# Retention and a two-layer MLP in one kernel: q and k loaded by GpSimd ahead of the weights, v from SyncE, k cast by VectorE, token groups of 512 and 256, first group alone

## Chip, cores, metric

One core of a Trainium2 chip. The metric is the device time of one execution in microseconds (us); medians of several runs are quoted. Names in profile lines: PE is TensorE, DVE VectorE, ACT ScalarE, POOL GpSimd, SP SyncE; L178 is line 178 of that run's kernel, so one statement has different line numbers in different kernels.

## The reference

```python
# q, k, v: (8 batches, 8 heads, 576 tokens, 64)
scores = (1/8) * q @ k^T                       # per batch and head
ret    = scores * gamma[h] ** (i - j)  for i >= j, else 0
x      = (ret @ v) as (4608 tokens, 512)
h      = x @ w_in                              # 512 x 2048
out    = max(0.01 * h, h) @ w_out              # 2048 x 512
```

Inputs and output are f32; the kernel computes in f16 with f32 sums.

## The kernel before

The attention part works on 40 *units*: 128 tokens of one batch (64 for the last of each batch), all 8 heads. Its steps are short, and they are dealt out between the long blocks of the two MLP layers. VectorE lays v and k out block-diagonally (`vdiag`, `kstk`), PE transposes q and k (`tr`; VectorE and ScalarE copy k from there into `kdiag`), and states (`ups`, `sinit`, `sdiag`), scores (`sc`, `s`) and outputs (`ot`) follow. ScalarE copies each output into `xT`, the input of the first MLP layer, whose matmuls write `hps`; those of the second write `yps`.

```python
def load(u):                       # q and k, f32, from SyncE
    for x, t_ap in enumerate((q, k)):
        t = ld_pool.tile([P, H, D], FP, name=f"qk32_{x}")    # 4 buffers
        nc.sync.dma_start(out=t[0:n], in_=...)

def load_v(b):                     # v of a whole batch, cast to f16 by the DMA, 8 DMAs
    nc.gpsimd.dma_start(out=t[...], in_=v[b, ...])

def cast(u):                       # q and k to f16, times decay table
    for x in range(2):
        eng = nc.vector if (u < 5 and x == 1) else nc.gpsimd
        eng.tensor_tensor(out=t[0:n], in0=qk32[u, x][0:n], in1=<table>, op=MUL)

def st_transpose(u):
    <2 vdiag copies, 4 kstk copies, on VectorE, f16 SBUF to SBUF>
    <8 transposes on PE; qT and half of kdiag on ScalarE; half of kdiag on VectorE>

def s0():                          # first step of unit u
    load(u + 4)
    if w == 1: load_v(b + 1)
    cast(u + 2)
    st_transpose(u)
# further steps: st_state(u, 0), st_scores(u), st_state(u, 1), st_out(u)
...
# start: load(0), load_v(0), load(1..3), cast(0), cast(1), then 4 w_in and 4 w_out
# loads on GpSimd (f32 to f16). Nine groups of 512 tokens: group g's first layer runs
# beside group g-1's second layer and the units of group g+1.
```

Of the kernel before, what the change touches and what calls it, by code (L numbers as in the profile page):

```python
# [10 lines left out]
FP = mybir.dt.float32  # L11
F16 = mybir.dt.float16
# [6 lines left out]
def kernel(  # L19
# [16 lines left out]
    nc = tc.nc  # L36
    B, H, S, D = q.shape
    NT, DM = out.shape
    DFF = moe_w_in.shape[1]
    P = 128  # L40
    CH = 64
    BLK = 3 * CH
    NP = H // 2
    NI = S // CH
    NF = DFF // P
    TOK = 512
    NG = NT // TOK
# [18 lines left out]

    const_pool = ctx.enter_context(tc.tile_pool(name="const", bufs=1))
    ld_pool = ctx.enter_context(tc.tile_pool(name="ld", bufs=4))
    v_pool = ctx.enter_context(tc.tile_pool(name="vp", bufs=2))
    a_pool = ctx.enter_context(tc.tile_pool(name="ap", bufs=3))  # L70
    g_pool = ctx.enter_context(tc.tile_pool(name="gp", bufs=2))
    o_pool = ctx.enter_context(tc.tile_pool(name="op", bufs=4))
    tr_pool = ctx.enter_context(tc.tile_pool(name="trp", bufs=1, space=PSUM))
# [3 lines left out]
    h_pool = ctx.enter_context(tc.tile_pool(name="hpp", bufs=2, space=PSUM))  # L77
    y_pool = ctx.enter_context(tc.tile_pool(name="yp", bufs=2, space=PSUM))
# [12 lines left out]
    xT = const_pool.tile([P, NP, NT], F16, name="xT")  # L91
    w_in16 = const_pool.tile([P, NP, DFF], F16, name="w_in16")
    w_out16 = const_pool.tile([P, NF, DM], F16, name="w_out16")

    NZ = 2
# [4 lines left out]
    sdiags = [const_pool.tile([P, NP, P], F16, name=f"sdiag{z}") for z in range(NS)]  # L100
    halves = [const_pool.tile([P, H, D], F16, name=f"half{x}") for x in range(2)]

    vst = {}

    def load_v(b):
        t = v_pool.tile([P, NP, NI, D], F16, name="vst")
        vst[b] = t
        for p in range(NP):
            for hh in range(2):
                nc.gpsimd.dma_start(  # L110
                    out=t[CH * hh : CH * hh + CH, p, :, :],
                    in_=v[b, 2 * p + hh].rearrange("(i s) d -> s i d", s=CH),
                )

    units = [(b, w) for b in range(B) for w in range((S + P - 1) // P)]
    NU = len(units)
    nrows = [min(P, S - P * w) for b, w in units]
    qk32 = {}
    qk16 = {}

    def load(u):
        b, w = units[u]
        n = nrows[u]
        for x, t_ap in enumerate((q, k)):
            t = ld_pool.tile([P, H, D], FP, name=f"qk32_{x}")
            qk32[u, x] = t
            nc.sync.dma_start(
                out=t[0:n],
                in_=t_ap[b, :, P * w : P * w + n, :].rearrange("h t d -> t h d"),
            )  # L130

    def cast(u):
        b, w = units[u]
        n = nrows[u]
        for x in range(2):
            if n == P:
                t = a_pool.tile([P, H, D], F16, name=f"qk16_{x}")
            else:
                t = halves[x]
            qk16[u, x] = t  # L140
            eng = nc.vector if (u < 5 and x == 1) else nc.gpsimd
            eng.tensor_tensor(  # L142
                out=t[0:n],
                in0=qk32[u, x][0:n],
                in1=tab_sb[0:n, w % 3, x, :].unsqueeze(2).to_broadcast([n, H, D]),
                op=MUL,
            )

    qTs = {}
    s16s = {}  # L150
# [5 lines left out]
    def st_transpose(u):  # L156
        b, w = units[u]
        n = nrows[u]
        nb = n // CH
        z = u % NZ  # L160
        for hh in range(2):
            nc.vector.tensor_copy(  # L162
                out=vdiags[z][CH * hh : CH * hh + CH, :, 0:nb, CH * hh : CH * hh + CH],
                in_=vst[b][CH * hh : CH * hh + CH, :, 2 * w : 2 * w + nb, :],
            )
        k16 = qk16[u, 1].rearrange("s (p h) d -> s p h d", h=2)
        if not (w == 4):
            for j in range(nb):
                for hh in range(2):
                    nc.vector.tensor_copy(  # L170
                        out=kstks[z][CH * hh : CH * hh + CH, :, j, CH * hh : CH * hh + CH],
                        in_=k16[CH * j : CH * j + CH, :, hh, :],
                    )
        tr = tr_pool.tile([P, 2, NP, P], F16, name="tr")
        for x in range(2):
            for p in range(NP):
                nc.tensor.transpose(  # L177
                    tr[:, x, p, :],  # L178
                    qk16[u, x][:, 2 * p : 2 * p + 2, :].rearrange("t h d -> t (h d)"),
                    ident,  # L180
                )
        qT = a_pool.tile([P, NP, P], F16, name="qT")
        qTs[u] = qT
        nc.scalar.copy(out=qT[:, :, 0:n], in_=tr[:, 0, :, 0:n])  # L184
        for hh, eng in ((0, nc.scalar.copy), (1, nc.vector.tensor_copy)):
            eng(  # L186
                out=kdiags[z][CH * hh : CH * hh + CH, :, 0:nb, CH * hh : CH * hh + CH],
                in_=tr[CH * hh : CH * hh + CH, 1, :, 0:n].rearrange(
                    "e p (j c) -> e p j c", c=CH
                ),  # L190
            )

    def st_state(u, j):
        b, w = units[u]
        z = u % NZ
# [6 lines left out]
        for p in range(NP):  # L202
            nc.tensor.matmul(  # L203
                out=ut[:, p, :],
                lhsT=kstks[z][:, p, j, :],
                rhs=vst[b][:, p, i, :],
                start=(i % 3 == 0 and p == 0),
                stop=(i % 3 == 2),
                skip_group_check=True,
            )  # L210
# [54 lines left out]
    def st_out(u):  # L265
# [19 lines left out]
        t0 = b * S + P * w  # L285
        nc.scalar.copy(out=xT[:, :, t0 : t0 + n], in_=ot[:, :, 0:n])  # L286

    def slots(u):

        b, w = units[u]  # L290

        def s0():
            if u + 4 < NU:
                load(u + 4)
            if w == 1 and b + 1 < B:
                load_v(b + 1)
            if u + 2 < NU:
                cast(u + 2)
            st_transpose(u)

        yield s0
        yield lambda: st_state(u, 0)
        yield lambda: st_scores(u)
        if nrows[u] == P:
            yield lambda: st_state(u, 1)
        yield lambda: st_out(u)
# [7 lines left out]
        nc.vector.memset(sdiags[z], 0.0)  # L314
    for x in range(2):
        nc.vector.memset(halves[x], 0.0)
    load(0)
    load_v(0)
    for u in range(1, 4):
        load(u)  # L320
    cast(0)
    cast(1)
    FQ = DFF // 4
# [8 lines left out]
            in_=moe_w_out[c * FQ : (c + 1) * FQ, :].rearrange("(c k) f -> k c f", k=P),  # L332
        )

    first_slot = []
    need = []
    for u in range(NU):
        b, w = units[u]
        lo = b * NI + 2 * w
        for s in slots(u):  # L340
            first_slot.append(s)
            need.append(lo // 8)
    done = 0

    g_tiles = {}

    def g1(g, fc):
        if fc == 0:
            g_tiles[g] = g_pool.tile([P, NF, TOK], F16, name="gt")
        hps = h_pool.tile([P, TOK], FP, name="hps")  # L350
        for c in range(NP):
            nc.tensor.matmul(  # L352
                out=hps,
                lhsT=w_in16[:, c, fc * P : (fc + 1) * P],
                rhs=xT[:, c, g * TOK : (g + 1) * TOK],
                start=(c == 0),
                stop=(c == NP - 1),
            )
        nc.scalar.activation(  # L359
            out=g_tiles[g][:, fc, :], in_=hps,  # L360
            func=mybir.ActivationFunctionType.Lrelu,
        )

    y_cur = {}

    def g2(g, n):
        tb, part = n // 4, n % 4
        if part == 0:
            y_cur[g] = y_pool.tile([P, DM], FP, name="yps")
        for f in range(4 * part, 4 * part + 4):  # L370
            nc.tensor.matmul(  # L371
                out=y_cur[g],
                lhsT=g_tiles[g][:, f, tb * P : (tb + 1) * P],
                rhs=w_out16[:, f, :],
                start=(f == 0),
                stop=(f == NF - 1),
            )
        if part == 3:
            osb = o_pool.tile([P, DM], FP, name="osb")
            nc.vector.tensor_copy(out=osb, in_=y_cur[g])  # L380
            r0 = g * TOK + tb * P
            nc.sync.dma_start(out=out[r0 : r0 + P, :], in_=osb)

    def run_slots(upto):
        nonlocal done
        while done < upto:
            first_slot[done]()
            done += 1

    total = len(first_slot)  # L390
    ends = [sum(1 for x in need if x <= g) for g in range(NG)] + [total]
    run_slots(ends[0])
    for g in range(NG + 1):
        a = done
        e = ends[min(g + 1, NG)] if g < NG else total
        nblk = (16 if g < NG else 0) + (16 if g > 0 else 0)
        m = 0
        for n in range(NF):
            if g < NG:
                g1(g, n)  # L400
                m += 1
                run_slots(a + (e - a) * m // nblk)
            if g > 0:
                g2(g - 1, n)
                m += 1
                run_slots(a + (e - a) * m // nblk)


# [28 lines left out]
```

## Time and profile before

| | before |
|---|---|
| median of 3 runs | 366.6 us |
| span of the profiled run | 364.9 us |
| first matmul of the first MLP layer (hps) | 50.5 us |
| PE packed from | 81.4 us |
| VectorE busy | 198.1 us |

"Packed" means that PE waits for almost nothing: from 82 us to the end it waited 5.3 us. The prediction below shows the lines for this and how they are read. A line for a group of instructions has busy time in us and mean duration in ns behind the first bar, and the idle time before them behind the second.

### The profile page before, as it was taken

The page shows a single profiled execution, that of the slowest core. Times are in us where ns is not written, and L with a number is a line of the kernel's source. Part 1 is how long each engine was busy: PE and PEld are TensorE (multiplying, and loading weights), DVE is VectorE, ACT ScalarE, POOL GpSimd, SP SyncE. Part 2 cuts the span into 40 slices and gives each one's busy share as a digit, 9 for nine tenths or more (in the row PEclk, how much of TensorE's full clock was granted, in tenths as well). Part 3 has the DMA queues.
Part 4 walks back from the last instruction along what each step waited for, and adds up shares of the span by engine and source line. Part 5 has one row for each costly group of instructions (what it writes and reads, how often), then busy time and mean ns, then how long its engine had stood idle before and what let it go on. Part 6 is the DMA issues. An engine that isn't in the chain of part 4 may idle for free.

```text
span 364.9 us, 6523 instructions
## 1 busy us (share of the span) xinstructions
PE 311.6 (85%) x2560; PEld 168.9 (46%) x2560; DVE 198.1 (54%) x492; ACT 144.2 (40%) x266; POOL 131.4 (36%) x153
## 2 busy tenths in 40 slices
PE   0024278779999999999999999999999999999995
PEld 0023144445554555555555555555555455544442
DVE  5448248782656577636756775445884556300021
ACT  1111046354444455434444444444445444433300
POOL 9822379426322573166225822373132100000000
PEclk9999999899999999999999999999999999999999
DMA  9999999709335393387338943593452000011012
GB/s 158 189 196 196 176 192 182 126 3 78 91 78 128 90 189 89 88 118 93 86 88 156 125 103 77 129 152 88 105 113 73 31 29 32 29 44 44 29 62 84
DMA packets 122479, 37.71 MB, mean 103 GB/s; under 512 B 113744, under 2 KB 117840, under 8 KB 122448
## 3 DMA queue, kind: packets, MB, share of 16 engines
q1 hardware_dynamic: 80192, 28.32, 35.2%
q0 software_dynamic: 42112, 8.92, 27.3%
q8 instruction: 20, 0.33, 0.4%
q10 hardware_dynamic: 144, 0.06, 0.1%
q14 instruction: 11, 0.09, 0.1%
HBM read 36.76 MB, written 9.44 MB: 127 GB/s over the span
## 4 chain that ended last, share of the span: by engine, by line
PE 78%; DMA 7%; DVE 6%; POOL 4%; ACT 2%; issue 2%; POOLq 0%; DVEq 0%
PE yps L371 34%; PE hps L352 32%; DMA w_out<-in_moe_w_out_dram 7%; PE tr L177 4%; PE ot L275 2%; PE sc L242 2%; PE ot L280 2%; POOL vst L110 2%; PE ups L203 2%; ACT xT L286 1%; DVE kstk L170 1%; POOL qk L142 1%; POOL w_in L325 1%; DVE s L253 1%; DVE sdiag L233 1%
## 5 line engine op out<-in xcount | busy, mean ns | idle before, releaser
L352 PE MATMUL hps<-xT,w_in 128*128 128x512 f16 x576 | 149.9, 383 | 5.9 <-ACT xT L286 5.9
L371 PE MATMUL yps<-w_out,gt 128*128 128x512 f16 x576 | 145.2, 379 | 0.0
L359 ACT ACTIVATE gt<-hps 128x512 f16<-128x512 f32 x144 | 86.0, 597 | 133.0 <-PE hps L352 131.8
L142 POOL TENSOR_TENSOR qk<-qk,cs 128x512 f16<-128x512 f32 x60 | 62.5, 1059 | 117.0 <-DMA qk<-in_q_dram 39.5
L371 PEld LDWEIGHTS <-gt 128*128 128x128 f16 x576 | 52.8, 98 | 54.6
L352 PEld LDWEIGHTS <-w_in 128*128 128x128 f16 x576 | 51.0, 99 | 51.7 <-issue 8.1
L110 POOL DMA_DIRECT2D vst<-in_v_dram x64 | 47.5, 775 | 32.8 <-DMA w_out<-in_moe_w_out_dram 11.4
L380 DVE COPY osb<-yps 128x512 f32<-128x512 f32 x36 | 24.9, 691 | 51.3 <-PE yps L371 51.0
L186 DVE COPY kdiag<-tr 64x512 f16<-64x512 f16 (+1 forms) x40 | 16.0, 401 | 59.5 <-ACT kdiag L186 59.2
L286 ACT CAST xT<-ot 128x512 f16<-128x512 f32 (+1 forms) x40 | 21.6, 541 | 40.9 <-PE ot L280 40.9
L203 PE MATMUL ups<-vst,kstk 128*128 128x64 f16 x256 | 18.9, 199 | 21.1 <-DVE kstk L170 11.7
L170 DVE COPY kstk<-qk 64x256 f16<-64x256 f16 x128 | 34.2, 267 | 3.0
L177 PE MATMUL tr<-ident,qk 128*128 128x128 f16 x256 | 21.5, 232 | 15.8 <-POOL qk L142 15.8
L203 PEld LDWEIGHTS <-kstk 128*128 128x128 f16 x256 | 16.4, 102 | 35.6 <-DVE kstk L170 22.2
L184 ACT COPY qT<-tr 128x512 f16<-128x512 f16 (+1 forms) x40 | 21.6, 540 | 27.6 <-PE tr L177 27.6
L233 DVE TENSOR_TENSOR sdiag<-ups,sinit 64x256 f16<-64x256 f32 x64 | 26.9, 421 | 4.2 <-PE ups L203 3.3
L177 PEld LDWEIGHTS <-qk 128*128 128x128 f16 x256 | 18.2, 104 | 22.3 <-POOL qk L142 15.9
L162 DVE COPY vdiag<-vst 64x512 f16<-64x512 f16 (+1 forms) x80 | 27.0, 337 | 1.5
L253 DVE TENSOR_TENSOR s<-sc,cs 128x512 f16<-128x512 f32 x32 | 22.1, 691 | 9.0 <-PE sc L242 8.4
L275 PE MATMUL ot<-s,vdiag 128*128 128x64 f16 x288 | 23.0, 199 | 2.6 <-DVE s L253 2.6
L275 PEld LDWEIGHTS <-vdiag 128*128 128x128 f16 x288 | 20.9, 102 | 5.6 <-issue 1.0
L280 PE MATMUL ot<-qT,sdiag 128*128 128x64 f16 x256 | 22.0, 200 | 0.0
(30 smaller groups left out, 154.0 us busy)
## 6 DMA issues: line engine op xcount, KB each, us to landing
out_dram<-osb SPq DMA_DIRECT2D x36, 256.0 KB, 2.2
qk<-in_q_dram SPq DMA_DIRECT2D x32, 256.0 KB, 4.3
qk<-in_k_dram SPq DMA_DIRECT2D x32, 256.0 KB, 4.4
vst<-in_v_dram POOLq DMA_DIRECT2D x64, 72.0 KB, 5.0
w_in<-in_moe_w_in_dram POOLq DMA_DIRECT2D x4, 512.0 KB, 12.5
w_out<-in_moe_w_out_dram POOLq DMA_DIRECT2D x4, 512.0 KB, 23.3
qk<-in_q_dram SPq DMA_DIRECT2D x8, 128.0 KB, 4.7
qk<-in_k_dram SPq DMA_DIRECT2D x8, 128.0 KB, 4.4
```

Of the source, the lines that this page charges most:

```text
L110: nc.gpsimd.dma_start(out=t[CH * hh : CH * hh + CH, p, :, :], in_=v[b, 2 * p + hh].rearrange("(i s) d -> s i d", s=CH),)
L142: eng.tensor_tensor(out=t[0:n], in0=qk32[u, x][0:n], in1=tab_sb[0:n, w % 3, x, :].unsqueeze(2).to_broadcast([n, H, D]), op=MUL,)
L162: nc.vector.tensor_copy(out=vdiags[z][CH * hh : CH * hh + CH, :, 0:nb, CH * hh : CH * hh + CH], in_=vst[b][CH * hh : CH * hh + CH, :, 2 * ...
L170: nc.vector.tensor_copy(out=kstks[z][CH * hh : CH * hh + CH, :, j, CH * hh : CH * hh + CH], in_=k16[CH * j : CH * j + CH, :, hh, :],)
L177: nc.tensor.transpose(tr[:, x, p, :], qk16[u, x][:, 2 * p : 2 * p + 2, :].rearrange("t h d -> t (h d)"), ident,)
L203: nc.tensor.matmul(out=ut[:, p, :], lhsT=kstks[z][:, p, j, :], rhs=vst[b][:, p, i, :], start=(i % 3 == 0 and p == 0), stop=(i % 3 == 2), s ...
L233: nc.vector.tensor_tensor(out=dst, in0=ut[lo:hi], in1=sins[b][lo:hi], op=ADD)
L275: nc.tensor.matmul(out=o, lhsT=vdiags[z][:, p, j, :], rhs=s16s[u][:, p, j, :], start=True, stop=(i == 0),)
L280: nc.tensor.matmul(out=o, lhsT=sdiag_at[b, i][:, p, :], rhs=qTs[u][:, p, CH * j : CH * j + CH], start=False, stop=True,)
L352: nc.tensor.matmul(out=hps, lhsT=w_in16[:, c, fc * P : (fc + 1) * P], rhs=xT[:, c, g * TOK : (g + 1) * TOK], start=(c == 0), stop=(c == NP ...
L359: nc.scalar.activation(out=g_tiles[g][:, fc, :], in_=hps, func=mybir.ActivationFunctionType.Lrelu,)
L371: nc.tensor.matmul(out=y_cur[g], lhsT=g_tiles[g][:, f, tb * P : (tb + 1) * P], rhs=w_out16[:, f, :], start=(f == 0), stop=(f == NF - 1),)
```

## The change

The intent: let the first units' data come ahead of the 4.2 MB of weights, no longer block GpSimd behind the weight loads, and let the first 512 tokens go through both layers alone while the other loads arrive.

```diff
+    def load_qk(u):
...
-            nc.sync.dma_start(
+            nc.gpsimd.dma_start(
...
+    def load_v(u):                              # per unit, f32, four (or two) DMAs
+                nc.sync.dma_start(out=t[...], in_=v[b, ...])
...
     def cast(u):
-            eng = nc.vector if (u < 5 and x == 1) else nc.gpsimd
+            eng = nc.gpsimd if (u >= 4 and x == 0) else nc.vector
...
+        nc.scalar.copy(out=t[:, :, 0:nb, :], in_=v32[u][:, :, 0:nb, :])    # v to f16
...
+    def prepare(u):
+        if u + 2 < NU:
+            cast(u + 2)
+        if u + 4 < NU:
+            load_qk(u + 4)
+        if 4 <= u + 3 < NU:
+            load_v(u + 3)
+        st_transpose(u)

     def slots(u):
+        if u == 0:
+            yield lambda: prepare(0)
         yield lambda: st_state(u, 0)
         yield lambda: st_scores(u)
+        if u + 1 < NU:
+            yield lambda: prepare(u + 1)
         if nrows[u] == P:
             yield lambda: st_state(u, 1)
         yield lambda: st_out(u)
...
+    sizes = [512, 256, 256] + [512] * 6 + [256, 256]
...
+    run_steps(ends[0])
+    run(ends[0], g1_blocks(0))                  # first layer of the first group, alone
+    run(ends[1], g2_blocks(0, 2))               # its second layer, with units 4 to 6
+    run(ends[2], g1_blocks(1))
+    for g in range(2, NG):
+        run(ends[g + 1], g1_blocks(g), g2_blocks(g - 1))
+    run(ends[NG], g2_blocks(NG - 1))
```

The pool of f16 tiles also goes from 3 to 4 buffers.

More of the change, by code (lines that the diff above doesn't have):

```diff
@@ L68 @@
     ld_pool = ctx.enter_context(tc.tile_pool(name="ld", bufs=4))
-    v_pool = ctx.enter_context(tc.tile_pool(name="vp", bufs=2))
-    a_pool = ctx.enter_context(tc.tile_pool(name="ap", bufs=3))
+    a_pool = ctx.enter_context(tc.tile_pool(name="ap", bufs=4))
     g_pool = ctx.enter_context(tc.tile_pool(name="gp", bufs=2))
@@ L101 @@
     halves = [const_pool.tile([P, H, D], F16, name=f"half{x}") for x in range(2)]
-    vst = {}
-    def load_v(b):
-        t = v_pool.tile([P, NP, NI, D], F16, name="vst")
-        vst[b] = t
-        for p in range(NP):
-            for hh in range(2):
-                nc.gpsimd.dma_start(
-                    out=t[CH * hh : CH * hh + CH, p, :, :],
-                    in_=v[b, 2 * p + hh].rearrange("(i s) d -> s i d", s=CH),
-                )
     units = [(b, w) for b in range(B) for w in range((S + P - 1) // P)]
@@ L119 @@
     qk16 = {}
-    def load(u):
+    v32 = {}
+    vst = {}
+    def load_qk(u):
         b, w = units[u]
@@ L130, in load @@
             )
+    def load_v(u):
+        b, w = units[u]
+        t = ld_pool.tile([P, NP, 2, D], FP, name="v32")
+        v32[u] = t
+        for j in range(nrows[u] // CH):
+            t0 = P * w + CH * j
+            for hh in range(2):
+                nc.sync.dma_start(
+                    out=t[CH * hh : CH * hh + CH, :, j, :],
+                    in_=v[b, :, t0 : t0 + CH, :].rearrange(
+                        "(p h) s d -> h s p d", h=2
+                    )[hh],
+                )
     def cast(u):
@@ L134, in cast @@
         n = nrows[u]
+        nb = n // CH
+        z = u % NZ
         for x in range(2):
@@ L147, in cast @@
             )
+        t = a_pool.tile([P, NP, 2, D], F16, name="vst")
+        vst[u] = t
+        nc.scalar.copy(out=t[:, :, 0:nb, :], in_=v32[u][:, :, 0:nb, :])
     qTs = {}
@@ L163, in st_transpose @@
                 out=vdiags[z][CH * hh : CH * hh + CH, :, 0:nb, CH * hh : CH * hh + CH],
-                in_=vst[b][CH * hh : CH * hh + CH, :, 2 * w : 2 * w + nb, :],
+                in_=vst[u][CH * hh : CH * hh + CH, :, 0:nb, :],
             )
@@ L205, in st_state @@
                 lhsT=kstks[z][:, p, j, :],
-                rhs=vst[b][:, p, i, :],
+                rhs=vst[u][:, p, j, :],
                 start=(i % 3 == 0 and p == 0),
@@ L286, in st_out @@
         nc.scalar.copy(out=xT[:, :, t0 : t0 + n], in_=ot[:, :, 0:n])
-    def slots(u):
-        b, w = units[u]
-        def s0():
-            if u + 4 < NU:
-                load(u + 4)
-            if w == 1 and b + 1 < B:
-                load_v(b + 1)
-            if u + 2 < NU:
-                cast(u + 2)
-            st_transpose(u)
-        yield s0
+    def prepare(u):
[6 more added lines that the diff above has]
+        st_transpose(u)
+    def slots(u):
+        if u == 0:
+            yield lambda: prepare(0)
         yield lambda: st_state(u, 0)
         yield lambda: st_scores(u)
+        if u + 1 < NU:
+            yield lambda: prepare(u + 1)
         if nrows[u] == P:
@@ L316 @@
         nc.vector.memset(halves[x], 0.0)
-    load(0)
-    load_v(0)
-    for u in range(1, 4):
-        load(u)
+    for u in range(4):
+        load_qk(u)
+        load_v(u)
     cast(0)
@@ L333 @@
         )
-    first_slot = []
+    sizes = [512, 256, 256] + [512] * 6 + [256, 256]
+    starts = [sum(sizes[:g]) for g in range(len(sizes))]
+    NG = len(sizes)
+    steps = []
     need = []
@@ L338 @@
         b, w = units[u]
-        lo = b * NI + 2 * w
+        lo = b * S + P * w
         for s in slots(u):
-            first_slot.append(s)
-            need.append(lo // 8)
+            steps.append(s)
+            need.append(max(g for g in range(NG) if starts[g] <= lo))
+    ends = [sum(1 for x in need if x <= g) for g in range(NG)]
+    ends += [ends[-1]] * 2
     done = 0
-    g_tiles = {}
-    def g1(g, fc):
-        if fc == 0:
-            g_tiles[g] = g_pool.tile([P, NF, TOK], F16, name="gt")
-        hps = h_pool.tile([P, TOK], FP, name="hps")
-        for c in range(NP):
-            nc.tensor.matmul(
-                out=hps,
-                lhsT=w_in16[:, c, fc * P : (fc + 1) * P],
-                rhs=xT[:, c, g * TOK : (g + 1) * TOK],
-                start=(c == 0),
-                stop=(c == NP - 1),
-            )
-        nc.scalar.activation(
-            out=g_tiles[g][:, fc, :], in_=hps,
-            func=mybir.ActivationFunctionType.Lrelu,
-        )
@@ L364 @@
-    y_cur = {}
-    def g2(g, n):
-        tb, part = n // 4, n % 4
-        if part == 0:
-            y_cur[g] = y_pool.tile([P, DM], FP, name="yps")
-        for f in range(4 * part, 4 * part + 4):
-            nc.tensor.matmul(
-                out=y_cur[g],
-                lhsT=g_tiles[g][:, f, tb * P : (tb + 1) * P],
-                rhs=w_out16[:, f, :],
-                start=(f == 0),
-                stop=(f == NF - 1),
-            )
-        if part == 3:
-            osb = o_pool.tile([P, DM], FP, name="osb")
-            nc.vector.tensor_copy(out=osb, in_=y_cur[g])
-            r0 = g * TOK + tb * P
-            nc.sync.dma_start(out=out[r0 : r0 + P, :], in_=osb)
@@ L384, in run_slots, with run_steps @@
-    def run_slots(upto):
+    def run_steps(upto):
         nonlocal done
         while done < upto:
-            first_slot[done]()
+            steps[done]()
             done += 1
-    total = len(first_slot)
-    ends = [sum(1 for x in need if x <= g) for g in range(NG)] + [total]
-    run_slots(ends[0])
-    for g in range(NG + 1):
-        a = done
-        e = ends[min(g + 1, NG)] if g < NG else total
-        nblk = (16 if g < NG else 0) + (16 if g > 0 else 0)
-        m = 0
-        for n in range(NF):
-            if g < NG:
-                g1(g, n)
-                m += 1
-                run_slots(a + (e - a) * m // nblk)
-            if g > 0:
-                g2(g - 1, n)
-                m += 1
-                run_slots(a + (e - a) * m // nblk)
+    g_tiles = {}
@@ new lines, with g1_blocks, block @@
+    y_cur = {}
+    def g1_blocks(g):
+        tok, t0 = sizes[g], starts[g]
+        nf = TOK // tok
+        def block(fb):
+            if fb == 0:
+                g_tiles[g] = g_pool.tile([P, NF, tok], F16, name=f"gt{tok}")
+            hps = h_pool.tile([P, nf, tok], FP, name="hps")
+            for f in range(nf):
+                fc = fb * nf + f
+                for c in range(NP):
+                    nc.tensor.matmul(
+                        out=hps[:, f, :],
+                        lhsT=w_in16[:, c, fc * P : (fc + 1) * P],
+                        rhs=xT[:, c, t0 : t0 + tok],
+                        start=(c == 0),
+                        stop=(c == NP - 1),
+                    )
+            nc.scalar.activation(
+                out=g_tiles[g][:, fb * nf : (fb + 1) * nf, :], in_=hps,
+                func=mybir.ActivationFunctionType.Lrelu,
+            )
+        return [lambda fb=fb: block(fb) for fb in range(NF // nf)]
@@ new lines, in g2_blocks, with block @@
+    def g2_blocks(g, width=1):
+        t0 = starts[g]
+        def block(tbs, part):
+            for f in range(4 * part, 4 * part + 4):
+                for tb in tbs:
+                    if f == 0:
+                        y_cur[g, tb] = y_pool.tile([P, DM], FP, name="yps")
+                    nc.tensor.matmul(
+                        out=y_cur[g, tb],
+                        lhsT=g_tiles[g][:, f, tb * P : (tb + 1) * P],
+                        rhs=w_out16[:, f, :],
+                        start=(f == 0),
+                        stop=(f == NF - 1),
+                    )
+            if part == 3:
+                for tb in tbs:
+                    osb = o_pool.tile([P, DM], FP, name="osb")
+                    nc.vector.tensor_copy(out=osb, in_=y_cur[g, tb])
+                    r0 = t0 + tb * P
+                    nc.sync.dma_start(out=out[r0 : r0 + P, :], in_=osb)
+        return [
+            lambda tb=tb, part=part: block(range(tb, tb + width), part)
+            for tb in range(0, sizes[g] // P, width)
+            for part in range(4)
+        ]
@@ new lines, in run @@
+    def run(upto, *lists):
+        order = sorted(
+            ((n + 0.5) / len(ls), x, n) for x, ls in enumerate(lists) for n in range(len(ls))
+        )
+        a = done
+        for m, (_, x, n) in enumerate(order):
+            lists[x][n]()
+            run_steps(a + (upto - a) * (m + 1) // len(order))
+    run_steps(ends[0])
[4 more added lines that the diff above has]
+        run(ends[g + 1], g1_blocks(g), g2_blocks(g - 1))
```

## The prediction

> **What bounds the kernel now**
>
> I first read the busy rows of the page, which cut the span into 40 slices of 9.12 us.
>
> ```profile
> PE   0024278779999999999999999999999999999995
> PEclk9999999899999999999999999999999999999999
> DMA  9999999709335393387338943593452000011012
> ```
>
> PE is full from the ninth slice on; before that it is mostly idle, while the DMA row is full for seven slices. So there are two stages: a start that waits for data, and some 280 us of packed matmuls. How packed they are, the waits of PE from 82 us to the end tell:
>
> ```profile
> PE hps L352 <- ACT xT L286: 4.5, 7, 0.7
> PE ups L203 <- DVE kstk L170: 0.8, 1, 0.8
> ```
>
> 5.3 us in 280 us: nothing but less matmul time can shorten this stage. The change keeps the arithmetic, so what it can win lies ahead of 82 us. Next PE and GpSimd in order of time:
>
> ```profile
> 44.58 1.03 PE L177 MATMUL tr<-ident,qk 128*128 128x128 f16 x8 [7.18 <-POOL qk L142]
> 50.54 1.87 PE L352 MATMUL hps<-xT,w_in 128*128 128x512 f16 x4 [0.67 <-ACT xT L286]
> ```
>
> ```profile
> 18.31 0.80 POOL L110 DMA_DIRECT2D vst<-in_v_dram  x1 [1.53 <-DMA w_in<-in_moe_w_in_dram]
> 42.72 0.73 POOL L110 DMA_DIRECT2D vst<-in_v_dram  x1 [2.84 <-DMA w_out<-in_moe_w_out_dram]
> 43.47 1.05 POOL L142 TENSOR_TENSOR qk<-qk,cs 128x512 f16<-128x512 f32 x1
> ```
>
> The first layer's first matmul is at 50.54 us, after unit 3. (A unit is 128 tokens of one batch, 64 for the last of each batch; 40 in all.) Unit 3 waited for a q cast on GpSimd at 43.47, and that stood behind eight v loads of batch 1, each of which waited for one weight load to land: the listing of the instructions shows eight semaphores in rotation for GpSimd's DMAs, so the ninth waits for the first. From 50.5 to 80.8 us PE does 16 blocks of the first layer (13.8 us at 0.863 per four matmuls) and five units, with stalls on VectorE, where GpSimd's casts stretch the copies (0.58 and 0.94 us undisturbed):
>
> ```profile
> 60.99 2.34 DVE L162 COPY vdiag<-vst 64x512 f16<-64x512 f16 x2
> 63.35 2.46 DVE L170 COPY kstk<-qk 64x256 f16<-64x256 f16 x4
> ```
>
> **What the Trainium skill says**
>
> "DMA: Bandwidth & Descriptors", section "Queues, rings and completion order": on each DMA engine one ring is consumed in order, and the engine goes round between the rows that have work, packet by packet. The trace agrees: between 15 and 42 us, each 2.5 us hold 382 weight packets (1 KB, 96 ns each) and 385 q/k packets (256 B); and the first batch-1 v load, issued at 18.31, landed 25.6 us later, behind all the weights.
> The same page, "Issuing engines are not separate DMA queues": all issuers share 16 engines, so moving q, k to GpSimd and v to SyncE creates no bandwidth. The trace agrees so far as 190 GB/s is the plateau whichever queue is in front.
> "SBUF — State Buffer", "SBUF: two separate sides": VectorE and GpSimd lock one port pair for whole instructions, and VectorE can starve GpSimd's descriptor writing. The stretched copies above agree for casts; beside bare DMA issues (54 to 60 us) the same copies took 0.80 and 1.36, a milder effect. How much 80 q/k issues on GpSimd suffer, no run here shows yet.
>
> **The change part by part**
>
> *Loads.* q, k of units 0 to 3 (8 DMAs, 8192 rows of 256 B) stand ahead of the eight weight DMAs in GpSimd's ring; v comes from SyncE as f32 (1024 rows per unit). This removes GpSimd's block behind the weights. But q, k of unit 4 on are then behind all 4.19 MB of weights.
>
> *Who needs them when.* The order of VectorE's instructions in the changed build is what decides. `prepare(u+1)` now sits inside unit u and begins with the casts of u+3, k always on VectorE. So VectorE reaches the cast of k(4) before it has copied anything of unit 2, and before the last state copies of unit 1; the cast of k(5) stands in unit 2, that of k(6) in unit 3 before the copies that its output needs. VectorE is in order, so the first group cannot go through the first layer before k(4), k(5) and k(6) have landed, behind the weights. The plan "first group alone while the rest loads" is undone by casts two units ahead.
>
> *When k(4) lands.* Ahead of it: 8192 rows of q, k and up to 7680 rows of v (units 0 to 7; SyncE runs ahead as soon as ScalarE frees its buffers), 4.06 MB. Before read 11,300 such rows (2.9 MB) in 11.5 us, 252 GB/s: 16 us, so to 19 us. Weights: 4096 packets; alone, at 85 to 96 ns over 16 engines (a pair took 104.7 ns, of which a lone 256 B row is some 20), 22 to 24.6 us: to 41 to 44. Then 1024 rows of unit 4 and the receipt, 2 to 2.5 us: 45 us, give or take 2. k(6) follows 6 us later.
>
> *From there to the first layer.* VectorE's work by measured durations: rest of unit 1 0.84; unit 2: cast 0.68, vdiag 0.58, kstk 0.90, kdiag 0.43, state 2.6, s 0.69 ; unit 3 nearly the same; unit 4 cast-ahead and copies 1.4: 12.6 us in all. Unit 1 of before (26.21 to 30.76 us) ran its VectorE chain almost without gaps; I add 2.5 us for waits and for port locks, and 1.3 for output matmuls and the xT copy. First layer's start: 45 + 16.4, about 61 us, against 50.5.
>
> *First group alone.* Layer one 13.8 us, plus 1 for a clock that starts low (first four matmuls of before: 1.87 us instead of 0.86). Layer two 13.8 + 3.3 us of units 4 to 6, with two dependent steps after every 1.7 us block: 18.6. Group 1 (256 tokens): 6.9 + two units, whose VectorE work (5.2 us each, cast included) is more than PE's 9.7: 12. Next stage, 256 and 256 tokens: 13.8 + 4.9 of PE, 18.9 + locks of VectorE: 20.5. Sum 66, to 127 us.
>
> *The rest.* First layer 3584 tokens (7 times 13.8), second 3840 (7.5 times), 21 full units at 1.38 us and 6 half ones at 0.75: 97 + 104 + 33.5 = 234, plus six boundaries of 0.7: 238.5. To 365.5; tail as before (3.9 from the last matmul), and 1.7 from the span to the measured time: 371. The same sum for before, from 80.8 us: 273.4 + 5.3 = 278.7, to 359.5, when the last matmul ended at 361, so the method is good to about 2 us.
>
> *Off the path.* 256-token groups halve the moving columns: a 256-column matmul (0.11 us) still covers the next weight load, as 64-column ones at 0.03 us each show, so PE loses nothing. VectorE gains 35 k casts (24 us), ScalarE 40 v casts (22 us), GpSimd loses as many casts and 64 v issues, and gains 80 q/k issues; all remain under 70% in the packed stage.
>
> **Rivals**
>
> 1. *The start is earlier.* If units 2 and 3 were not held, unit 3 would be done near 30 us and the end near 340. For it: GpSimd's 25 us block is really gone, and the design aims at it. Against it: VectorE's order and the in-order ring. A milder form: packets of the plain GpSimd loads run better than the 128 B cast rows, k(4) lands at 40 and VectorE sees less of the port lock (one GpSimd cast per unit, not two): first layer at 54, packed from there: some 360 to 363.
> 2. *The two effects cancel.* First layer 8 us later, but then no gaps, where before lost 10 us to stalls between 50 and 81: 365 to 369. Half in my sum already.
> 3. *GpSimd's descriptors become the bound.* 80 issues of 1024 rows each, starved by VectorE: loads arrive late in the packed stage too, PE gets holes: 380 and over. Against it: a load is issued two units, some 15 us, before its cast, and an issue of 576 rows took 0.78 us.
>
> **Range and chances**
>
> My sum says 371; the milder form of the first rival and the cancelling one pull lower, the third pulls up. I put 369, with 358 to 379 for 8 in 10. Faster by over 2% (below 359.3) needs the weights not to hold units 2 and 3: 0.15. Slower by over 2% (above 373.9) needs the first layer after 63 us or a starved packed stage: 0.27. Within: 0.58.
>
> **What would show it**
>
> Right: a gap of VectorE of about 15 us or more ahead of the cast of k(4), ended by a q/k DMA, at 43 to 47 us; the first hps matmul near 60; then 16 blocks without a gap; PE packed from some 127 us. Wrong: first hps matmul before 45 us, or VectorE idle ahead of that cast only briefly (rival 1); idle PE behind GpSimd or q/k DMAs after 130 us (rival 3); packed PE already from 80 us.

## More of the kernel before

```profile
L170 DVE COPY kstk<-qk 64x256 f16<-64x256 f16 x128 | 34.2, 267 | 3.0
```

Each such copy takes 0.222 us when nothing disturbs it, so 34.2 us for 128 is not much above the 28.4 of undisturbed ones. VectorE is busy 54% of the span.

## The result

The changed kernel takes 398.25 us (median of 4 runs, 397.2 to 399.2), the kernel before 366.18 in the same rounds: ratio 1.087, interval 1.083 to 1.092. A ratio is the mean time of one kernel's fast runs over the mean of the other's of the same rounds, so not quite the ratio of the medians. The change made the kernel 8.7% slower; the predicted range ended at 379.

The busy rows of the changed kernel, in 40 slices of 9.9 us (tenths of a slice):

```profile
PE   1022048987797679789999998999999999999996
DVE  6442493077879897997698789766897743532111
DMA  7999972025463535714534464345342201010102
```

PE does not stay full after the first layers start; from the 9th to the 18th slice, to some 178 us, it has holes, and in those slices VectorE is at 7 to 9 tenths. What PE waited for between 150 and 200 us (us in total, times, longest):

```profile
PE ups L211 <- DVE sdiag L239: 2.9, 1, 2.9
PE ups L211 <- DVE sdiag L241: 1.4, 1, 1.4
PE hps L380 <- ACT xT L294: 0.7, 1, 0.7
PE ups L211 <- DVE kstk L178: 0.4, 1, 0.4
```

VectorE makes `sdiag` after the kstk copies of the unit that it prepares, so what stretches those copies delays it.

The start, in order of time on VectorE and on PE (start, duration, what; in brackets the idle time before it and what ended it):

```profile
45.04 0.74 DVE L147 TENSOR_TENSOR half<-qk,cs 64x512 f16<-64x512 f32 x1 [11.14 <-DMA qk<-in_k_dram]
```

```profile
62.41 15.05 PE L380 MATMUL hps<-xT,w_in 128*128 128x512 f16 x64 [0.67 <-ACT xT L294]
```

That is the predicted start to 1.4 us: VectorE stands 11.1 us before the cast of k(4), which lands at 45 us, and the first layer begins at 62.4 (predicted 61). The new thing is later. The group of kstk copies:

```profile
L178 DVE COPY kstk<-qk 64x256 f16<-64x256 f16 x128 | 72.7, 568 | 2.7
```

The same 128 copies of the same shape take 72.7 us instead of 34.2. An ordinary stretch in time, first VectorE, then GpSimd:

```profile
199.24 2.83 DVE L178 COPY kstk<-qk 64x256 f16<-64x256 f16 x4
...
206.18 0.67 DVE L147 TENSOR_TENSOR half<-qk,cs 64x512 f16<-64x512 f32 x1
206.78 0.58 DVE L170 COPY vdiag<-vst 64x512 f16<-64x512 f16 x2
207.40 2.62 DVE L178 COPY kstk<-qk 64x256 f16<-64x256 f16 x4
```

```profile
199.01 0.88 POOL L116 DMA_DIRECT2D qk<-in_k_dram  x1 [4.49 <-DVE vdiag L170]
199.91 1.05 POOL L147 TENSOR_TENSOR qk<-qk,cs 128x512 f16<-128x512 f32 x1
200.89 0.92 POOL L116 DMA_DIRECT2D qk<-in_q_dram  x1
207.16 0.88 POOL L116 DMA_DIRECT2D qk<-in_k_dram  x1 [5.34 <-DVE half L147]
208.06 1.05 POOL L147 TENSOR_TENSOR qk<-qk,cs 128x512 f16<-128x512 f32 x1
```

In each unit GpSimd stands still until something of VectorE ends, and then it works for 2.9 us: a k load, the q cast, a q load. The kstk copies of VectorE fall exactly into these 2.9 us. I matched every kstk copy of the trace against GpSimd's instructions (overlaps under 0.03 us left out):

| kstk copies | before: number, mean us | changed: number, mean us |
|---|---|---|
| beside nothing on GpSimd | 109, 0.222 | 44, 0.223 |
| beside a DMA issue only | 11, 0.295 | 57, 0.330 |
| beside a cast (and perhaps an issue) | 8, 0.85 | 27, 1.63 |

Before had 75 casts on GpSimd and 8 copies beside one; the changed kernel has 36 casts and 27 copies beside one. Of those 27, 26 took 0.95 us or more, and each of the 26 ended 0.08 to 0.10 us after the cast beside it: they were held until it was over. What GpSimd waits for, over the whole run (us in total, times, longest):

```profile
POOL qk L116 <- DVE qk L147: 72.8, 13, 18.0
POOL qk L116 <- DVE vdiag L170: 53.1, 12, 5.8
POOL qk L116 <- DVE half L147: 33.4, 6, 6.4
```

These are waits of the k load for a free f32 buffer of k. With four buffers, k of unit u+4 goes where k of unit u was, and that becomes free when VectorE has cast it. The trace bears this out: from 61 us on, each of these k loads began 0.29 to 0.32 us after the end of a k cast on VectorE; where the profile names vdiag, it is only the copy that ran in between. VectorE's next work in program order after that cast are the copies of another unit. So the cast that moved to VectorE now fires GpSimd's burst at the worst place.

How the loss divides, by the first hps matmul of each group (all from the traces; "1st, 2nd, 3rd, 4th group" are those of 512, 256, 256 and 512 tokens; the last column is the end of the last matmul):

| us | 1st | 2nd | 3rd | 4th | last matmul |
|---|---|---|---|---|---|
| predicted | 61 | | | 127 | 365.5 |
| changed | 62.4 | 101.5 | 116.0 | 143.1 | 391.6 |
| with the copies first (first experiment below) | 57.0 | 92.2 | 104.9 | 127.2 | 366.2 |

Against the prediction: 1.4 us at the start, 14.7 between the first and the fourth group, 10.0 after that. Not all of the second figure need be VectorE: the granted clock of the profiled run was 0.94 between 62 and 143 us, and 1.00 with the copies first (57 to 127 us). What that is worth is not separated.

### The profile page after: what moved, and what is told of

It reads as the page before. It is cut to its first block, busy times and chain, and to the rows that moved or that the text cites. A ratio compares the mean times of both kernels' runs of the same rounds, so it can differ in the third digit from the quotient of the medians.

```text
span 395.4 us, 6875 instructions
## 1 busy us (share of the span) xinstructions
PE 316.1 (80%) x2688; PEld 183.2 (46%) x2688; DVE 251.4 (64%) x531; ACT 163.6 (41%) x306; POOL 111.8 (28%) x130
## 4 chain that ended last, share of the span: by engine, by line
PE 60%; DVE 20%; DMA 10%; issue 4%; ACT 2%; POOL 2%; SPq 1%; POOLq 0%; ACTq 0%; DVEq 0%
PE yps L403 26%; PE hps L380 26%; DVE kstk L178 8%; DMA qk<-in_k_dram 5%; DMA w_in<-in_moe_w_in_dram 3%; PE tr L185 2%; POOL qk L116 2%; PE sc L250 2%; PE ups L211 2%; DVE s L261 2%; DVE kdiag L194 2%; DVE osb L413 2%; DMA v<-in_v_dram 1%; DVE sdiag L239 1%; DVE qk L147 1%
## 5 line engine op out<-in xcount | busy, mean ns | idle before, releaser
L380 PE MATMUL hps<-xT,w_in 128*128 128x512 f16 (+1 forms) x704 | 148.0, 345 | 6.7 <-ACT xT L294 6.7
L403 PE MATMUL yps<-w_out,gt 128*128 128x512 f16 x576 | 146.9, 383 | 0.4 <-DVE osb L413 0.4
L380 PEld LDWEIGHTS <-w_in 128*128 128x128 f16 x704 | 64.9, 99 | 50.5 <-issue 9.1
L116 POOL DMA_DIRECT2D qk<-in_k_dram x40 | 33.9, 848 | 161.6 <-DVE qk L147 70.2
L178 DVE COPY kstk<-qk 64x256 f16<-64x256 f16 x128 | 72.7, 568 | 2.7
L211 PEld LDWEIGHTS <-kstk 128*128 128x128 f16 x256 | 16.5, 102 | 65.9 <-DVE kstk L178 30.5
L116 POOL DMA_DIRECT2D qk<-in_q_dram x40 | 35.3, 882 | 5.2 <-DVE qk L147 2.6
L155 ACT CAST vst<-v 128x512 f16<-128x512 f32 (+1 forms) x40 | 22.8, 570 | 21.8 <-DMA v<-in_v_dram 21.6
L147 POOL TENSOR_TENSOR qk<-qk,cs 128x512 f16<-128x512 f32 x28 | 29.5, 1054 | 2.1 <-DMA qk<-in_q_dram 1.7
L147 DVE TENSOR_TENSOR qk<-qk,cs 128x512 f16<-128x512 f32 x36 | 24.5, 683 | 5.4 <-DMA qk<-in_k_dram 2.9
L268 DVE TENSOR_TENSOR s<-sc,cs 128x256 f16<-128x256 f32 x8 | 3.4, 425 | 32.8 <-PE sc L250 32.8
```

What stands on the lines that cost most here:

```text
L116: nc.gpsimd.dma_start(out=t[0:n], in_=t_ap[b, :, P * w : P * w + n, :].rearrange("h t d -> t h d"),)
L147: eng.tensor_tensor(out=t[0:n], in0=qk32[u, x][0:n], in1=tab_sb[0:n, w % 3, x, :].unsqueeze(2).to_broadcast([n, H, D]), op=MUL,)
L178: nc.vector.tensor_copy(out=kstks[z][CH * hh : CH * hh + CH, :, j, CH * hh : CH * hh + CH], in_=k16[CH * j : CH * j + CH, :, hh, :],)
L211: nc.tensor.matmul(out=ut[:, p, :], lhsT=kstks[z][:, p, j, :], rhs=vst[u][:, p, j, :], start=(i % 3 == 0 and p == 0), stop=(i % 3 == 2), s ...
L380: nc.tensor.matmul(out=hps[:, f, :], lhsT=w_in16[:, c, fc * P : (fc + 1) * P], rhs=xT[:, c, t0 : t0 + tok], start=(c == 0), stop=(c == NP ...
L403: nc.tensor.matmul(out=y_cur[g, tb], lhsT=g_tiles[g][:, f, tb * P : (tb + 1) * P], rhs=w_out16[:, f, :], start=(f == 0), stop=(f == NF - 1),)
```

## The experiments

Each is an edit of the changed kernel unless another base is named; all results were correct. Four theories: **A**, the GpSimd cast, fired by VectorE's own cast, locks the port that the kstk copies need; **B**, VectorE just got too much work (24 us of k casts); **C**, the new groups crowd PE; **D**, it is GpSimd's DMA issues, not its casts.

### Copies ahead of the casts

```diff
 def prepare(u):
+    st_copies(u)                  # vdiag and kstk of this unit, taken out of st_transpose
     cast(u + 2)
     load_qk(u + 4)
     load_v(u + 3)
     st_transpose(u)               # without the copies
```

> Edit: in each prepare step VectorE does the vdiag and kstk copies of this unit before the k cast of two units later; same instructions on the same engines. Theory A (the k cast on VectorE frees a k buffer, which releases GpSimd's k load, q cast and q load just when VectorE does kstk, and the port lock of the GpSimd cast stops it): kstk falls from 72.7 us busy to below 45, PE is packed from 130 us on, time 372 to 382. Theory B (VectorE is simply loaded by the 24 us of added k casts, whatever their place): kstk may fall but the time stays above 390. Theory C (the new groups leave PE waiting in the early stages): above 390 too. First hps matmul at 60 to 62 us in all of them.

Measured: 371.7 us (ratio to before 1.016, 1.013 to 1.019). The kstk group:

```profile
L178 DVE COPY kstk<-qk 64x256 f16<-64x256 f16 x128 | 28.7, 224 | 2.7
```

And the same burst of GpSimd with what VectorE does meanwhile:

```profile
195.42 0.69 POOL L116 DMA_DIRECT2D qk<-in_k_dram  x1 [6.50 <-DVE qk L147]
196.12 1.06 POOL L147 TENSOR_TENSOR qk<-qk,cs 128x512 f16<-128x512 f32 x1
197.10 0.93 POOL L116 DMA_DIRECT2D qk<-in_q_dram  x1
```

```profile
193.46 0.94 DVE L178 COPY kstk<-qk 64x256 f16<-64x256 f16 x4
194.43 0.69 DVE L147 TENSOR_TENSOR qk<-qk,cs 128x512 f16<-128x512 f32 x1
195.16 0.43 DVE L200 COPY kdiag<-tr 64x512 f16<-64x512 f16 x1
195.61 0.42 DVE L236 TENSOR_TENSOR stmp<-ups,sinit 128x256 f32<-128x256 f32 x1
196.07 1.39 DVE L237 TENSOR_TENSOR sinit<-stmp,cs 128x256 f32<-128x256 f32 x1
```

GpSimd is still fired by VectorE's cast, but the copies are over by then, and operations that read PSUM (TensorE's result memory; kdiag, stmp) keep their duration. Only sinit, whose two inputs are in SBUF, is held (1.39 us; 0.43 undisturbed), and it comes once per batch (held in 6 of 8). No kstk copy lies beside a cast any more. The order of instructions alone was worth some 26 us: the same work on the same engines. B and C, which expected above 390, fall. The start came 5.4 us earlier, which I had not expected. Between the cast of k(4) and the first layer, VectorE's instructions were stretched by some 4.3 us in the changed kernel (four kstk copies took 2.64 us at 46.6 us, a sinit 1.43) and by 0.5 here, and the copies of unit 2 (1.5 us) now run in the wait ahead of that cast.

### k casts back to GpSimd

```diff
-            eng = nc.gpsimd if (u >= 4 and x == 0) else nc.vector
+            eng = nc.gpsimd if (u >= 4 and (x == 0 or u >= 5)) else nc.vector
```

> Edit: k casts of unit 5 on go back to GpSimd, as in the kernel before; all else as changed. Theory A: GpSimd frees its own k buffers, so its bursts are no longer tied to VectorE's cast; though it now has two casts per unit, kstk falls to 35 to 55 us busy; VectorE loses 24 us as well; 372 to 382. Theory B: kstk stays near 70 us and the time falls by the removed 24 us of casts at most, to 380 to 388. Theory C: above 390.

Measured: 381.4 us (ratio 1.043, 1.041 to 1.044), kstk 40.9 us. VectorE's sum fell from 251.4 to 212.7 us, 38.7 us: more than the 24 of casts. A's expectation for kstk holds, and the time is inside its window. But 24 vdiag copies now lay beside casts (vdiag 35.6 us, 23.3 in the changed kernel), and the first layer began at 65.9 us. Untying the two engines goes with a gain of 16.8 us; two casts per unit, at places that nobody chose, still hit. It is 9.7 us worse than one cast at a harmless place.

### Later q and k from SyncE

```diff
-            nc.gpsimd.dma_start(
+            (nc.gpsimd if u < 4 else nc.sync).dma_start(
```

> Edit: q and k of units 4 on are loaded from SyncE; units 0 to 3 stay ahead of the weights on GpSimd. Theory A: GpSimd's q cast is then started by a landing, some 4 us after the cast on VectorE, past kstk; kstk below 50 us. Theory D (it is GpSimd's DMA issues that stop VectorE, not its casts): kstk below 40, as no issue is left. The start: q, k of unit 4 no longer queue behind all weights but share one ring with v, beside the weights at some 150 rows per us; first hps matmul 50 to 62 us. Time 370 to 385.

Measured: 376.2 us (ratio 1.028, 1.026 to 1.030), kstk 35.0 us with 12 copies beside a cast, first layer at 58.3 us. Both A and D allow this; the next but one tells them apart. The load of k(4), no longer behind all the weights in a ring, brought the start forward by 4 us only: it was cast at 34.3 us instead of 45.0, but now ScalarE's v cast of unit 4, also in order and two units ahead, waited 15.6 us for its data, until 45.2, and the first group's kdiag copies stood behind it.

### Late casts

No cast of units 4 to 6, and no preparation of unit 4, before the output of unit 3:

```diff
-        cast(u + 2)
+        for c in {2: [], 3: [], 4: [4, 5, 6]}.get(u, [u + 2]): cast(c)
...
-        if u == 0:
+        if u in (0, 4):
             yield lambda: prepare(u)
...
-        if u + 1 < NU:
+        if u + 1 < NU and u != 3:
             yield lambda: prepare(u + 1)
```

> Edit: the casts of units 4, 5, 6 and all preparation of unit 4 come after the output of unit 3, so nothing of the first group waits for loads behind the weights. Theory of the start (VectorE's in-order cast of k(4) held the first group): first hps matmul at 43 to 48 us instead of 62.4, and the time falls by 12 to 17, to 381 to 386. Rival (the start is hidden, because VectorE is the bound until 250 us and gives it back): first hps earlier, but the time falls by less than 5.

Measured: 381.9 us (ratio 1.044, 1.042 to 1.045), kstk unchanged at 71.2 us. The first layer:

```profile
45.28 16.28 PE L381 MATMUL hps<-xT,w_in 128*128 128x512 f16 x64 [0.67 <-DMA qk<-in_q_dram]
```

17 us earlier, and 16.3 us of it reached the end. The in-order cast on VectorE did hold the first group, as predicted; it was a second, separate cost.

### q casts to VectorE too

```diff
-            eng = nc.gpsimd if (u >= 4 and x == 0) else nc.vector
+            eng = nc.vector
```

> Edit to the changed kernel alone: the q casts from unit 4 on move from GpSimd to VectorE, too, so GpSimd does nothing but issue DMAs. This adds 36 casts, 24 us, to the busiest engine. Theory A (the GpSimd cast holds the port, an issue hardly does): kstk falls from 72.7 to 30 to 42 us, VectorE's sum from 251 to 232 to 242, and the time falls by 6 to 18 us, to 380 to 392, though the busiest engine got more work. Theory B (load of VectorE): 405 to 420. Theory D (the DMA issues block): kstk stays above 60 and the time rises.

Measured: 385.6 us (ratio to before 1.054, 1.052 to 1.057). GpSimd now only issues DMAs, and the kstk group is

```profile
L178 DVE COPY kstk<-qk 64x256 f16<-64x256 f16 x128 | 38.7, 302 | 2.7
```

63 of the 128 copies lie beside an issue and take 0.384 us on average; the other 65 take 0.223. VectorE got 36 casts more, and its sum fell from 251.4 to 241.6 us; the kernel became 12.6 us faster by loading the engine that PE waits for. So the cast is the cost (1.63 us per copy hit) and an issue costs a little (0.33 to 0.38 instead of 0.22). D falls, and B once more. Load is not free for all that: this version is 13.9 us slower than the one with the copies first, and its VectorE is busy 26 us longer; the two differ in more than load, so its price is not shown by itself.

### Late casts and copies first together

```diff
 def prepare(u):
+    if u == 4: cast(4)
+    st_copies(u)
-    cast(u + 2)
+    for c in {2: [], 3: [], 4: [5, 6]}.get(u, [u + 2]): cast(c)
```

and the steps of unit 4 as in the late casts.

> Edit: both former edits at once, copies ahead of the casts and no casts of units 4 to 6 before the output of unit 3. If port lock and held start are two separate costs, their gains add: 371.7 less the 16 us of the late casts, 353 to 359, with kstk below 35 us busy and the first hps matmul at 43 to 47 us. If they overlap (VectorE's stretched copies also made up the late start), only part: 360 to 368.

Measured: 361.8 us (ratio 0.989, 0.986 to 0.992), kstk 30.5 us, first layer at 45.4 us. That is short of 353 to 359: of the 16 us of the late casts about 10 remain. The start is 45.4 us with or without undisturbed copies, so the 5.4 us by which the copies alone had brought the start forward are in both gains and cannot be had twice. The window for overlapping gains (360 to 368) is where it fell.

### The old groups, with the copies first

```diff
-    sizes = [512, 256, 256] + [512] * 6 + [256, 256]
+    sizes = [512] * 9
...
-    run(ends[0], g1_blocks(0))
-    run(ends[1], g2_blocks(0, 2))
-    run(ends[2], g1_blocks(1))
-    for g in range(2, NG):
+    run(ends[1], g1_blocks(0))
+    for g in range(1, NG):
```

> Edit: copies ahead of the casts, and token groups as before: nine of 512, the first one interleaved with the units of the second. It asks what the new groups are worth with the port lock gone. Theory C (the new groups cost by themselves: short groups crowd PE with dependent steps): faster than the 371.7 us of copies first alone, by 3 to 8 us. Rival (they are neutral or help a start that is held by loads): 371 to 380.

Measured: 371.7 us, as with the new groups (371.7). C falls; the groups are neutral as long as the start is held.

### Weights held until v has landed

With late casts and copies first as the base, one small GpSimd copy ahead of the weight loads:

```diff
+    nc.gpsimd.tensor_copy(out=hold_t, in_=v32[3][:, :, :, 0:1])
     for c in range(4):            # w_in, w_out
```

> Edit: as both edits at once, and a small GpSimd copy out of the last v tile of unit 3 ahead of the weight loads, so that the weights start only when v of the first group has landed. In the changed kernel ScalarE waits for v until 21 us, as its 256 B rows take turns packet by packet with the far longer packets of q and k and then with the weights. If that wait is what keeps unit 0 to 23 us, the first hps matmul comes at 35 to 40 us and the time at 343 to 352. Rival (units 0 to 3 are bound by VectorE's chain, or the weights come later by as much): within 3 us of both edits alone.

Measured: 357.7 us (ratio 0.977, 0.974 to 0.979), the first version more than 2% ahead of the kernel before. What it aimed at, in the changed kernel's ScalarE:

```profile
21.98 0.62 ACT L155 CAST vst<-v 128x512 f16<-128x512 f32 x1 [8.19 <-DMA v<-in_v_dram]
28.76 0.62 ACT L155 CAST vst<-v 128x512 f16<-128x512 f32 x1 [5.20 <-DMA v<-in_v_dram]
```

The third and fourth v cast waited until 22.0 and 28.8 us (21.4 and 28.2 in the base of this experiment); here they came at 17.9 and 19.4, and the first layer began at 40.6 instead of 45.4. The window (35 to 40 us, 343 to 352) was missed: between 29.8 and 39.6 us VectorE idles less than 1 us, so the units are bound by its own chain there, and my window for the total rested on the unreached sum of the experiment before.

### The old groups, in that version

> Edit: copies first, late casts and held weights as in the fastest so far (357.7), with nine groups of 512 and the second group's units beside the first group's first layer. Theory: the first group alone through both layers is worth something only while loads of unit 4 on are missing; they land at 45 to 56 us, so with the old groups PE meets unit 4 at about 42 us and stalls: 357 to 365. Rival (VectorE's idle 10 us during the first group alone are the dearer thing): 347 to 355.

The edit is that of the old groups above. Measured: 369.9 us (ratio 1.009, 1.005 to 1.012), 12.2 us slower than with the new groups; the first theory allowed a loss of up to 7 us, so its direction held and its size did not. First layer at 40.8 us, and then the waits of PE up to 120 us begin with

```profile
PE tr L191 <- POOL half L147: 7.4, 1, 7.4
```

The transposes of unit 4 wait for its q cast and so for data that follow the weights. With an early start the new groups are worth 12 us; with a held start (the experiment two above) nothing.

### Units 4 and 5 beside the end of the first layer

```diff
-    run(ends[0], g1_blocks(0))
+    g1_0 = g1_blocks(0)
+    run(ends[0], g1_0[:10])
+    run(ends[0] + 5, g1_0[10:])
```

> Edit: the fastest so far, with the first five steps of units 4 and 5 placed after the blocks 10 to 16 of the first group's first layer instead of behind it. In the trace of the fastest so far VectorE idles from 39.6 to 57.5 us but for one cast, as the ScalarE copy of v and PE's transposes of unit 4 stand behind that layer, and then is the bound until 113 us. If idle VectorE time there is what the early stages lack, this saves 4 to 7 us: 350 to 354. If the loads (k of unit 4 at 49 us, units 5 and 6 later) are the bound: 356 to 359.

Measured: 356.8 us (ratio to before 0.976, 0.971 to 0.980; without the edit 0.977, 0.974 to 0.979). No difference that can be told from noise. The fourth group began at 111.7 instead of 113.0 us, but the second layer of the first group began 2.4 us later, after a wait of 1.45 us for unit 4's kdiag and at a clock of 0.89 between 40 and 57 us (1.00 without the edit). The time misses the window of idle VectorE time and lies in that of the loads, but the edit had this cost of its own, so neither theory is shown.

## Why the prediction was wrong

*Right.* The bound of the kernel before; that the packed stage has nothing to lose but stalls; that VectorE's in-order casts would put the first group behind the weights, k(4) at 45 us and the first layer at 61 (62.4 measured; the mechanism was right, the closeness is partly luck, as VectorE's own work on that path was some 10.8 us where 12.6 were summed, and its waits and stretched instructions 4.8 where 2.5 were added); the 16 blocks without a gap after it; the tail (3.9 us predicted; the last matmul ends at 391.6, the span at 395.4); that 256-token groups cost PE nothing (with the copies first, both groupings take 371.7 us, and from the fourth group to the end of the matmuls pass 239.0 us where 238.5 were summed).

*The step that failed.* It is the term for port locks (VectorE held up by GpSimd) in the sums of "first group alone", and with it the statement that all engines "remain under 70% in the packed stage". I had put kstk at 0.90 us per unit and added one or two microseconds per stage for locks, as in the trace of before. Measured: 2.6 to 2.8 us for the four copies of an ordinary unit, 72.7 us for all. VectorE was 83% busy between 150 and 250 us (59% before), not under 70%. That is 14.7 us too little in the early stages, of which the first experiment gives back 10.5, and 10.0 us too little in the packed stage, of which it gives back 9.5. The remaining 4.2 us of the early stages are spread over its three stages (1.8, 0.7 and 1.8 us, the table's times with the copies first against the prediction's sums); their cause is not shown.

*Why it was mis-sized.* I counted the casts ("one GpSimd cast per unit, not two") and took fewer casts for fewer collisions. The collisions depend on when a cast starts. I had read VectorE's order in the changed build, but the prediction does not ask what GpSimd's k loads wait for now: the k cast on VectorE frees a buffer, GpSimd starts, and VectorE's next instructions are copies of the kind that the lock holds. 26 of 36 casts hit a kstk copy, against 6 of 75 before.

*The rivals.* The third named a time of 380 and over, but by another way: GpSimd starved, PE waiting for late loads. Nothing of it shows: after 62 us PE waits for VectorE and, at the starts of groups, for ScalarE's xT copy, not for GpSimd or DMAs. It was VectorE that was held. The first rival, an early start, was reached only by the versions with late casts.

*The range.* 358 to 379 held the version without the collision (371.7, where the sum was 371 and the point 369), not the kernel as written. That 371.7 lies so near the sum is partly luck: its first layer began 4.0 us earlier than predicted, and its early stages took 4.2 us longer.

## What to carry to other kernels

A buffer that becomes free is a starting gun: for every engine that waits for one, look at what the engine that frees it does in the next few microseconds, and whether the two share a port. Moving work between engines can cost more by the new moment of the other engine's work than by the work moved; reordering two independent groups of instructions was worth some 26 us here, and adding 36 casts to the engine that PE waited for made the kernel 12.6 us faster. And parts of a change may be worth nothing until another part is mended: the new groups gained 0 us with a held start and 12 us with an early one.

## What the Trainium skill lacked or had wrong

- "SBUF — State Buffer", "SBUF: two separate sides" states the lock and that the loser blocks for the whole instruction. A 0.222 us copy beside a GpSimd cast took 1.69 us on average (26 cases) and ended 0.08 to 0.10 us after it. 24 of the 26 had started before the cast, by up to 0.67 us, beside the DMA issue ahead of it, and were not let through between the two; so the copies lost more than the 1.05 us of the cast alone. PSUM-reading copies (kdiag, 0.43 us) kept their time; a two-input SBUF operation was held (sinit 1.39 us).
- For DMAs issued by GpSimd, that page describes VectorE holding up the descriptor writing and gives no size for the reverse. Here the reverse is mild: copies beside a plain q or k issue took 0.33 to 0.38 us instead of 0.22.
- No page says that a buffer's release can fall into step with the copies that the lock holds; 26 of 36 casts did.
- "DMA: Bandwidth & Descriptors", "SWDGE vs HWDGE vs iDMA" gives packets of preferably up to 4096 B for DMAs issued by GpSimd. The trace agrees for plain q, k loads of 256 B rows (4608 packets of 4 KB, 256 ns each), but not for casting ones: v in the kernel before was recorded as 36,864 packets of 128 B (32 ns each), the weights as 4096 of 1 KB (96 ns). Nothing there says what turns by packet mean for a queue of single 256 B rows beside longer packets: the third v tile was cast at 21.4 us, and at 17.9 when the 1 KB packets of the weights were held back (both with late casts and copies first).
